# Where the products with v stand: ahead of the next quad's scores instead of behind the row maxima

## The chip, the cores and the metric

The kernel runs on one core of one Trainium2 chip. The metric is the device time of one launch in microseconds, lower is better. Three timed runs of the kernel before gave 1579.79, 1580.98 and 1583.72 us; the median is 1580.98 us. The engines are called TensorE (PE, its weight load PEld), VectorE (DVE), ScalarE (ACT), GpSimd (POOL) and SyncE (SP, which only issues DMAs here).

## The reference

Two layers with the same weights, each made of an attention block and a feed-forward block, in float32, over 2048 rows of 640:

```
x = x + attn(layernorm(x));  x = x + ffn(layernorm(x))      # twice
attn: q, k, v = split(x @ wqkv);  32 heads of 20
      p = softmax(q k^T / sqrt(20), with 0 <= i - j < 256);  (p v) @ wo
ffn:  relu(x @ w1 + b1)^2 @ w2 + b2,   inner size 1536
```

The mask is a sliding window of 256 keys, so a block of 256 queries needs its own keys and those of the block before.

## The kernel before

**Units.** The work is cut into 16 units: 8 blocks of 256 rows in each of 2 layers (`NU` = 16, unit `u`). Large products take each operand as two float16 parts, high and low, and sum three products (`mm3`, L327); this is the dense work. Per unit there are four dense stages: q and k (`stage_qk`), v (`stage_v`), the output projection (`stage_o`) and the feed-forward block (`stage_f`). In unit `u` the kernel runs the attention of unit `u` and, between its parts, the dense stages of others: q, k and v of unit `u + 1`, the output projection and feed-forward block of unit `u - 1`. The last two units have no q, k and v of a later unit left over, so a part of the dense work is held back for them: 18 us of it go from unit 14 to unit 15 (`CARRY`), 20 us from unit 15 to the end (`KEEP`), by the planner's own reckoning.

**Attention.** The 32 heads of a unit are taken four at a time, a quad; a unit has 8 (`NQ`), `n` counts them through all units. Each quad has three runs of small matmuls:

- `max_quad(n)` (L653, in the first block of a layer L668): scores with queries in the partitions, into six PSUM banks `bb`. VectorE adds the mask and takes the maximum of each row (L633). Every second quad the maxima go back as extra rows of q: in most units through a transposing DMA (`max_cross`), in the first two through TensorE (`max_out`).
- `exp_quad(n)` (L757, in the first block L765): scores again with keys in the partitions and the maximum taken off by the extra rows, into the same six banks; ScalarE takes the exponentials (L779) into six buffers `pt`, and GpSimd sets what lies outside the window to zero (L794, L798).
- `pv_quad(n, quad)` (L828): the products of these weights with v, into one of the two PSUM banks that the dense work uses too (`mm_tile`, tag `mm`); ScalarE copies them out (L840), and after every second quad four DMAs on SP write them to the tensor `o` (L845). An extra column of v gives the sums of the weights.

The maxima run three quads ahead (`LEAD` = 3). The six banks `bb` are shared by the maxima and the scores: a run of either waits until the engine that reads the other's result is through (`bbjobs`).

**From `o` to the output projection.** After the first run of scores of unit `u`, `load_o(u - 1)` loads the unit before's `o` and sums from HBM (L871, L872), which waits for all its writes. VectorE divides by the sums (L904, L907), ScalarE and VectorE make the two float16 parts `od` (L911, L914), in four quarters, of which two let the first half of `stage_o` begin. `stage_o` stands in the dense work behind q and half of v.

**The order of the work.** It is written out by a planner that runs while the program is made. It keeps a clock of TensorE (`now`) and of each other engine, with costs in ns for each operation. An instruction of ScalarE, VectorE, GpSimd or SP is a `Job` with what it depends on and a priority; `pump` puts it into its engine's queue when the planner's clock has come to its start. So every engine, SP too, has a fixed order and waits in it. The dense work is a stream of pieces of about 0.5 us of matmuls; a `Want` in it (or before a run of attention) names jobs that must have ended, and by default also that one of the two `mm` banks is free.

`together` (L1104) merges attention and dense work in units 1 to 15. `turns` (L1071) yields two turns per quad: the first with weight 0.55 for the scores, the second with 0.45 for maxima and products with v (0.7 and 0.3 where no maxima are left). Before a turn, `work` (L1112) runs dense pieces until the share of the dense work due by then is done and the turn's wants have ended; if the dense stream itself must wait and the wants have ended, it goes on to the turn at once. With no wants given it has only the share to go by. After the last turn the rest of the dense work of the unit is run, but in units 14 and 15 what lies above the share is left for later. `flow` (L1168) does the same for unit 0: it takes a list of runs in order and puts a piece of dense work between them whenever the next one's wants have not ended.

After unit 15, `load_o(15)` and the unit's output projection, normalisation and feed-forward block follow, with what was kept of the dense work between them.

Of the kernel before, what the change touches and what calls it, by code (L numbers as in the profile page):

```python
# [26 lines left out]
NU = NL * NG  # L27
# [4 lines left out]
NQ = H // 4  # L32
# [13 lines left out]
def kernel(ctx: ExitStack, tc: tile.TileContext, x, wqkv, wo, w1, b1, w2, b2, out):  # L46
# [542 lines left out]
    GQ = NQ // 4  # L589
# [478 lines left out]
    LEAD = GQ + 1  # L1068
    late = []

    def turns(ns, ms, pace=0):  # L1071


        ms = [m for m in ms if m < NQ * NU]
        todo = list(ms)
        for q, n in enumerate(ns):
            m = todo.pop(0) if todo and (q + 1) * max(len(ms), pace) >= (len(ms) - len(todo) + 1) * len(ns) else None
            share = SHARE if m is not None else ALONE
            yield share, ("s", n), None
            yield 1 - share, ("v", n), m  # L1080
        for m in todo:
            yield 1.0, None, m
# [20 lines left out]

    def together(ns, ms, dense, cost, share=1.0, whole=True, after=None, pace=0):  # L1104

        ts = list(turns(ns, ms, pace))
        total = sum(t[0] for t in ts)
        done = part = 0.0
        quad = None
        s = Stream(dense)  # L1110
# [17 lines left out]
        for k, (part_, what, m) in enumerate(ts):  # L1128
            kind = what and what[0]
            wants = list(bbjobs)  # L1130
            if kind == "s" and what[1] % GQ == 0:
                wants.append(rowjobs[what[1] // NQ, what[1] % NQ // GQ])
            if m is not None:
                wants += [trips[m // NQ, j, m % NQ] for j in range(2)]
            if kind == "v":
                wants += quad[1][0]
            work(part, Want(*wants, bank=kind == "v"))
            if kind == "s":
                quad = exp_quad(what[1])
# [27 lines left out]

    def flow(todo, dense):  # L1168

        todo = list(todo)  # L1170
        quad = None
        while todo:
            kind, n = todo[0]
            u, G = n // NQ, n % NQ // GQ
            wants = {"m": [*bbjobs, trips.get((u, 0, n % NQ)), trips.get((u, 1, n % NQ))], "r": mxjobs.get((u, G), [None]),
                     "s": [*bbjobs, *([rowjobs.get((u, G))] if n % GQ == 0 else [])],
                     "v": quad[1][0] if quad else []}[kind]
            if not all(j is not None and j.end is not None and j.end <= now[0] + LOOK for j in wants):
# [13 lines left out]
            elif kind == "s":  # L1192
                quad = exp_quad(n)
# [51 lines left out]
    for u in range(1, NU):  # L1245
        last = u == NU - 1
# [13 lines left out]
        share = 1.0 - KEEP / cost if last else 1.0 - CARRY / cost if u == NU - 2 else 1.0  # L1260
        together(quads, ahead, dense, cost, share, u < NU - 2, after=(lambda: load_o(u - 1, last)) if u > 1 else None, pace=NQ)
    load_o(NU - 1, True)
# [31 lines left out]
```

## Time and profile before

| | |
|---|---|
| median of three timed runs | 1580.98 us (1579.79 to 1583.72) |
| the profiled execution, first to last instruction | 1580.5 us |
| its time beyond that span | not listed; the span lies 0.5 us under the median of the runs |
| TensorE busy | 1555.9 us, 98% |
| VectorE busy | 985.7 us, 62% |
| ScalarE busy | 733.6 us, 46% |
| GpSimd busy | 600.4 us, 38% |
| DMA | 160.44 MB, mean 102 GB/s |
| mean granted clock of TensorE | 0.996 |

In the rows of the profile "L327" is a line of the kernel; a row of the order in time gives start and duration in us, the engine, the line, the operation, what it writes and reads, how many instructions were merged, and in brackets the idle time before it and what ended it. In the list of waits the numbers are us in total, how often, and the longest. A row of a stretch of time, such as 113.90:124.10, gives the length of the stretch, then busy time and count for PE, PEld and, where they are shown, DVE, ACT and POOL, and at the end the granted clock, the share of DMA time and GB/s. Durations of matmuls overlap, so the time of a run is read from the start of one run to the start of the next. The chain of waits merges what ended last into pieces of start, duration, engine and line.

### The profile page before, as it was taken

The page shows a single profiled execution, that of the slowest core. Times are in us where ns is not written, and L with a number is a line of the kernel's source. Part 1 is how long each engine was busy: PE and PEld are TensorE (multiplying, and loading weights), DVE is VectorE, ACT ScalarE, POOL GpSimd, SP SyncE. Part 2 cuts the span into 40 slices and gives each one's busy share as a digit, 9 for nine tenths or more (in the row PEclk, how much of TensorE's full clock was granted, in tenths as well). Part 3 has the DMA queues.
Part 4 walks back from the last instruction along what each step waited for, and adds up shares of the span by engine and source line. Part 5 has one row for each costly group of instructions (what it writes and reads, how often), then busy time and mean ns, then how long its engine had stood idle before and what let it go on. Part 6 is the DMA issues. An engine that isn't in the chain of part 4 may idle for free. (4 is left out here: it accounts for less than half of the span.)

```text
span 1580.5 us, 52541 instructions
## 1 busy us (share of the span) xinstructions
PE 1555.9 (98%) x21570; PEld 1168.6 (74%) x21570; DVE 985.7 (62%) x3254; ACT 733.6 (46%) x1593; POOL 600.4 (38%) x1291
## 2 busy tenths in 40 slices
PE   8989999999999999999999999999999999999999
PEld 7666778777777777777777777777777777676777
DVE  8786765656756656565466756656665576656542
ACT  4565445444454444535444453444535445454522
POOL 1234434235253443524324252443524325344522
PEclk9999999999999999999999999999999999999999
DMA  9763344362533525344353533525354343532120
GB/s 277 200 183 103 78 111 86 100 129 51 123 88 103 112 56 127 79 121 94 89 128 67 123 88 103 112 57 131 76 125 88 89 110 70 124 88 58 30 67 18
DMA packets 243353, 160.44 MB, mean 102 GB/s; under 512 B 91176, under 2 KB 226856, under 8 KB 243112
## 3 DMA queue, kind: packets, MB, share of 16 engines
q1 hardware_dynamic: 236744, 147.58, 39.5%
q10 hardware_dynamic: 6368, 9.50, 2.1%
q8 instruction: 169, 2.77, 0.8%
q14 instruction: 72, 0.59, 0.1%
HBM read 84.68 MB, written 52.95 MB: 87 GB/s over the span
## 5 line engine op out<-in xcount | busy, mean ns | idle before, releaser
L779 ACT ACTIVATE pt<-bb 128x512 f32<-128x512 f32 (+1 forms) x736 | 375.9, 601 | 226.0 <-PE bb L757 198.5
L633 DVE CUSTOM_DVE_ANT_0 bb<-bb,maskq 128x320 f32<-128x320 f32 x896 | 409.2, 524 | 86.8 <-PE bb L653 74.6
L794 POOL TENSOR_SCALAR_AFFINE_SELECT pt<-pt 128x256 f32<-128x256 f32 x448 | 188.3, 422 | 562.7 <-ACT pt L779 549.8
L327 PE MATMUL acc<-y,w_s 128*128 128x256 f16 x2880 | 328.3, 273 | 0.5 <-DVE y L378 0.4
L327 PE MATMUL acc<-w_s,hh 128*128 128x320 f16 (+1 forms) x2340 | 326.4, 298 | 0.0
L327 PEld LDWEIGHTS <-w_s 128*128 128x128 f16 x2880 | 276.6, 98 | 52.1 <-issue 15.8
L327 PEld LDWEIGHTS <-hh 128*128 128x128 f16 x2340 | 222.1, 98 | 96.7 <-issue 11.5
L327 PEld LDWEIGHTS <-wq_s 128*128 128x128 f16 x2400 | 229.5, 98 | 46.1 <-issue 13.6
L327 PE MATMUL acc<-yT,wq_s 128*128 128x256 f16 x2250 | 258.6, 273 | 2.3 <-DVE qd L510 0.9
L798 POOL TENSOR_SCALAR_AFFINE_SELECT pt<-pt 128x256 f32<-128x256 f32 x512 | 213.6, 439 | 89.8 <-ACT pt L779 88.4
L1013 DVE TENSOR_TENSOR hh<-r,hh 128x256 f16<-128x256 f32 x192 | 95.4, 519 | 207.4 <-ACT hh L1010 200.4
L828 PE MATMUL pv<-pt,vt 128*32 128x128 f32 (+1 forms) x3840 | 189.8, 331 | 0.0
L1007 POOL TENSOR_TENSOR r<-r 128x256 f32<-128x256 f32 x192 | 114.2, 615 | 161.4 <-ACT r L1003 159.0
L840 ACT COPY ot<-pv 128x256 f32<-128x256 f32 x128 | 47.6, 372 | 267.0 <-PE pv L828 267.0
L327 PE MATMUL acc<-wo_s,od 128*128 128x320 f16 x960 | 141.6, 304 | 4.8 <-ACT od L911 3.0
L633 DVE DVE_READ_ACCUMULATOR2_ANT mx<- 128x1 f32 x1024 | 144.0, 141 | 0.0
L828 PEld LDWEIGHTS pv<-pt,vt 128*32 128x32 f32 x3840 | 105.5, 110 | 39.2 <-POOL pt L798 4.4
L327 PE MATMUL acc<-wq_s,yT 128*128 128x320 f16 x900 | 132.0, 300 | 1.4 <-DVE y L378 0.9
L327 PEld LDWEIGHTS <-od 128*128 128x128 f16 x960 | 91.9, 99 | 51.0 <-issue 6.4
L1003 ACT ACTIVATE r<-acc,b1s 128x256 f32<-128x256 f32 x192 | 80.5, 471 | 86.7 <-PE acc L327 85.4
L327 PEld LDWEIGHTS <-yT 128*128 128x128 f16 x900 | 85.7, 98 | 39.4 <-issue 6.7
L364 POOL TENSOR_TENSOR bmv<-bmv,neghalf 128x1 f32<-128x1 f32 x64 | 45.5, 717 | 135.8 <-DVE bmv L358 135.4
(95 smaller groups left out, 1226.1 us busy)
## 6 DMA issues: line engine op xcount, KB each, us to landing
qt<-qk SPq DMA_DIRECT2D x30, 480.0 KB
kt<-qk SPq DMA_DIRECT2D x30, 480.0 KB
qk<-qd SPq DMA_DIRECT2D x17, 640.0 KB
o<-ot SPq DMA_DIRECT2D x256, 42.0 KB
od<-o SPq DMA_DIRECT2D x14, 640.0 KB
qk<-yl SPq DMA_DIRECT2D x13, 640.0 KB
qk<-qd SPq DMA_DIRECT2D x17, 320.0 KB
xt<-in_A_x_dram SPq DMA_DIRECT2D x16, 320.0 KB
```

What stands on the lines that cost most here:

```text
L327: nc.tensor.matmul(acc, lhs(a, c), rhs(b, c), start=(k == 0), stop=(k == 3 * nk - 1))
L364: j = post("G", 520, lambda: nc.gpsimd.tensor_tensor(box["mv"][:, 3:4], box["mv"][:, 2:3], neghalf, op=ALU.pow), j, prio=prio)
L633: nc.vector.tensor_tensor_reduce(out=v, in0=v, in1=mask, scale=1.0, scalar=-3.0e38, op0=ALU.add, op1=ALU.max, accum_out=accum[e, w]),
L779: nc.scalar.activation(box["pt"][:, :o], bb[e][:, k, :o], AF.Exp, scale=SCALE / (QS * QS))
L794: nc.gpsimd.affine_select(out=m, in_=m, pattern=[[0, 2], [-1, P]], compare_op=ALU.is_gt, fill=0.0, base=0, channel_multiplier=1)
L798: nc.gpsimd.affine_select(out=m, in_=m, pattern=[[0, 2], [1, P]], compare_op=ALU.is_ge, fill=0.0, base=0, channel_multiplier=-1)
L828: nc.tensor.matmul(pv[32 * jj:32 * (jj + 1), q0 * P:(q0 + qn) * P], vf[:, c:c + 32], pj[:, j, :], start=(k == 0), stop=(k == len(steps) - ...
L840: nc.scalar.copy(ot[:, qd % 2], pv)
L1003: nc.scalar.activation(box["r"], acc[:, f, :], AF.Relu, bias=b1s[:, f0 + f:f0 + f + 1], scale=1.0 / (YS * WS))
L1007: nc.gpsimd.tensor_tensor(box["r"], box["r"], box["r"], op=ALU.mult)
L1013: nc.vector.tensor_sub(hh[:, 1, f, :], box["r"], hh[:, 0, f, :])
```

## The change

The products with v of a quad no longer belong to the turn of the maxima. In `together` they are held in a list `behind` and put out directly ahead of the next quad's scores, after one common wait: for the banks `bb`, for the maxima's rows, for all masks of the quad (before, for those of its first step), and for a free `mm` bank, which the turn of the maxima no longer asks for. The turn of the maxima now has no kind, so the block under `if what is None`, which runs dense work up to the share and then puts out waiting `max_out` calls, applies to it. The last quad of a unit is put out at the first turn of the next; in unit 14 it is put out at the unit's end (`flush`), and the last of unit 15 by `flow`. In unit 0 the list of runs names the products with v of quad `n - 1` ahead of the scores of `n`.

```diff
@@ turns
             share = SHARE if m is not None else ALONE
             yield share, ("s", n), None
-            yield 1 - share, ("v", n), m
+            yield 1 - share, None, m
@@ together(..., flush=False)
                 wants += [trips[m // NQ, j, m % NQ] for j in range(2)]
-            if kind == "v":
-                wants += quad[1][0]
-            work(part, Want(*wants, bank=kind == "v"))
+            values = kind == "s" and bool(behind)
+            if values:
+                wants += [j for ms in behind[0][1][1] for j in ms]
+            work(part, Want(*wants, bank=values))
             if kind == "s":
-                quad = exp_quad(what[1])
+                if values:
+                    pv_quad(*behind.pop())
+                behind.append((what[1], exp_quad(what[1])))
                 for it in late:
                     max_out(*it)
                 late.clear()
...
-            if kind == "v":
-                pv_quad(what[1], quad)
...
+        if flush:
+            work(part, Want(*(j for ms in behind[0][1][1] for j in ms)))
+            pv_quad(*behind.pop())
         work(part, None)
@@ flow(todo, dense, quad=None)
-                     "v": quad[1][0] if quad else []}[kind]
+                     "v": [j for ms in quad[1] for j in ms] if quad else []}[kind]
@@ unit 0
-        todo += [("s", n)] + ([("r", n + LEAD - GQ)] if n % GQ == 1 else []) + [("m", n + LEAD), ("v", n)]
+        todo += [("v", n - 1)] * (n > 0) + [("s", n)] + [("r", n + LEAD - GQ)] * (n % GQ == 1) + [("m", n + LEAD)]
+    todo += [("v", NQ - 1)]
@@ units 1 to 15
-        together(..., pace=NQ)
+        together(..., pace=NQ, flush=u == NU - 2)
+    n, quad = behind.pop()
+    flow([("v", n)], dense, quad)
     load_o(NU - 1, True)
```

More of the change, by code (lines that the diff above doesn't have):

```diff
@@ L1068 @@
     LEAD = GQ + 1
-    late = []
+    late, behind = [], []
     def turns(ns, ms, pace=0):
@@ L1102, in portion, with together @@
             yield c
-    def together(ns, ms, dense, cost, share=1.0, whole=True, after=None, pace=0):
+    def together(ns, ms, dense, cost, share=1.0, whole=True, after=None, pace=0, flush=False):
         ts = list(turns(ns, ms, pace))
@@ L1108, in together @@
         done = part = 0.0
-        quad = None
         s = Stream(dense)
@@ L1166, with flow @@
     QKC, VC, OC, FCST, LNC, CARRY, KEEP, MID = 16.4e3, 8.2e3, 8.2e3, 39.2e3, 1.2e3, 18e3, 20e3, 10e3
-    def flow(todo, dense):
+    def flow(todo, dense, quad=None):
         todo = list(todo)
-        quad = None
         while todo:
@@ L1260 @@
         share = 1.0 - KEEP / cost if last else 1.0 - CARRY / cost if u == NU - 2 else 1.0
-        together(quads, ahead, dense, cost, share, u < NU - 2, after=(lambda: load_o(u - 1, last)) if u > 1 else None, pace=NQ)
+        together(quads, ahead, dense, cost, share, u < NU - 2, after=(lambda: load_o(u - 1, last)) if u > 1 else None, pace=NQ, flush=u == NU - 2)
+    n, quad = behind.pop()
+    flow([("v", n)], dense, quad)
     load_o(NU - 1, True)
```

## The prediction

> **What bounds the kernel now.** I read the page first, then the list of waits, then the order in time of one inner quad, and at the end the last two units and the place where the clock falls.
>
> ```profile
> span 1580.5 us, 52541 instructions
> PE 1555.9 (98%) x21570; PEld 1168.6 (74%) x21570; DVE 985.7 (62%) x3254; ACT 733.6 (46%) x1593; POOL 600.4 (38%) x1291
> PEld pv L828 <- POOL pt L798: 4.4, 20, 0.4
> ```
>
> TensorE has 24.6 us without work in 1580.5. The wait that the change seems to aim at, products with v waiting for masked weights, is 4.4 us in 20 pieces of at most 0.4 us. So there is little to win; the question is whether the new order makes TensorE wait where it now does not. Below, s is a run of scores (L757), m a run of row maxima (L653), v the products with v (L828), "dense" all of L327. An inner quad:
>
> ```profile
> 590.79 0.75 PE L757 MATMUL bb<-qt,kt 62*64 62x192 f16 x32
> 591.63 3.05 ACT L779 ACTIVATE pt<-bb 128x512 f32<-128x512 f32 x6 [4.22 <-PE bb L757]
> 597.03 0.76 PE L653 MATMUL bb<-kt,qt 60*64 60x256 f16 x38
> 602.11 0.14 DVE L633 DVE_READ_ACCUMULATOR2_ANT mx<- 128x1 f32 x1
> 603.08 0.75 PE L757 MATMUL bb<-qt,kt 62*64 62x192 f16 x32
> 590.79:687.36 96.57, 74.85 (x595) 56.80 (x594) 1.00 0.44 97
> ```
>
> The cycle s to s is 12.29 us. It has two latencies: the exponentials end 3.89 us after s starts (then m may overwrite the six banks), and the last maximum is read 5.22 us after m starts (then s may). Both fit, because the planner spreads 595 dense matmuls over the unit's 96.57 us. Here the pace sets the order, not the latency. In the unit before the last (14) less is handed out, and it is the latency that sets it:
>
> ```profile
> 1418.78 0.75 PE L757 MATMUL bb<-qt,kt 62*64 62x192 f16 x32
> 1423.93 0.76 PE L653 MATMUL bb<-kt,qt 60*64 60x256 f16 x38
> 1424.62 1.51 PE L828 MATMUL pv<-pt,vt 128*32 128x256 f32 x32
> 1426.06 2.93 PE L327 MATMUL acc<-y,w_s 128*128 128x256 f16 x25
> 1428.47 0.14 DVE L633 DVE_READ_ACCUMULATOR2_ANT mx<- 128x1 f32 x1
> 1428.92 0.75 PE L757 MATMUL bb<-qt,kt 62*64 62x192 f16 x32
> 1354.04:1439.01 84.97, 61.11 (x495) 47.02 (x494) 1.00 0.38 91
> 1439.01:1511.10 72.09, 47.52 (x366) 34.37 (x365) 1.00 0.16 45
> 1511.10:1580.50 69.40, 64.54 (x540) 50.58 (x540) 1.00 0.15 48
> ```
>
> m to s takes 4.99 us, and s comes 0.31 us after the last maximum is read. Of these 4.99, v covers 1.44 (1424.62 to 1426.06). Unit 14 runs 495 of its 595 matmuls; the other 100 are the carry that covers unit 15 and the end.
>
> **The change, part by part.**
>
> The order itself. Each quad keeps its 32 + 38 + 32 small matmuls; m now goes over to dense, dense to v, v to s. The chain of waits holds this last order already, in the last quads, where no maxima are left:
>
> ```profile
> 1504.10 1.52 PE pv L828 x32
> ```
>
> v, between dense and s, costs 1.52 there against 1.44 in the inner quads. So 0.08 a quad at most, 9 us over 120 quads as an upper bound; but the starts of the runs show that what v gains after dense is lost in the dense run before it, and -0.5 to 2.5 us is left. I take **0**. The masks' wait goes, at most 4.4 us; its pieces are as long as the usual step between two kinds of weight load, so I take **0** here too.
>
> Inner units. [v, s] now go out together, once the maxima are read, the masks are through and a PSUM bank is free. Latency per quad: 3.89 + 5.22 + 1.44 + about 0.5 of rounding = 11.1 us, below 12.29. The pace covers it: **0**. If that cover were gone it would cost 1.44 us a quad. The first [v, s] of a unit brings the last v of the unit before some 4.6 us later against s, and with it the writes of o, their load and the chain to od. SP waits in order for these writes; the loads of x behind them are not urgent.
>
> ```profile
> 590.89 0.41 SPq L872 DMA_DIRECT2D od<-o  x1
> 596.20 0.54 DVE L904 RECIPROCAL rs<-rs 128x64 f32<-128x64 f32 x1
> 605.40 0.49 DVE L914 TENSOR_TENSOR od<-od 128x320 f16<-128x320 f32 x1
> 606.77 2.20 PE L327 MATMUL acc<-wo_s,od 128*128 128x320 f16 x15
> ```
>
> The slack is 606.77 - 605.89 = 0.88 us. Yet the chain stands behind the block of maxima (597 to 602.2) already; only the reciprocal of 0.54 us runs ahead of it. The load, landed by 596.2 now, lands by 600.8 then, still inside the block. So the chain loses 0.54 of 0.88: **0**. The loss if it doesn't hold is a rival below.
>
> First quad of unit 1. TensorE stands here for od, and v of this quad runs inside the hole:
>
> ```profile
> 112.39 0.27 PE L653 MATMUL bb<-kt,qt 60*64 60x256 f16 x1 [1.94 <-ACT pt L779]
> 113.56 2.54 PE L828 MATMUL pv<-pt,vt 128*32 128x256 f32 x32
> 118.38 7.14 PE L327 MATMUL acc<-wo_s,od 128*128 128x320 f16 x30 [2.27 <-ACT od L911]
> 611.03 4.25 PE L327 MATMUL acc<-wo_s,od 128*128 128x320 f16 x30
> 113.90:124.10 10.20, 7.92 (x53) 4.12 (x46) 8.65 (x28) 2.05 (x5) 0.85 (x3) 0.50 1.11 238
> ```
>
> In the new order this v comes with the next s, after the hole, and costs its 1.44 us: **+1.4** (0 to 2.5).
>
> Unit 14. v no longer covers the maxima, so dense fills all of it and then v delays s. From 4.99 the step m to s becomes 4.68 (maximum read) + 0.2 + 1.44 = 6.3: 1.3 us more, in seven of eight quads (after the eighth, v is put out ahead of unit 15 without waiting for the maxima), 9.2 us. Against it, m needs no bank any more. Two quads waited for one:
>
> ```profile
> 1354.73 5.09 PE L327 MATMUL acc<-yT,wq_s 128*128 128x256 f16 x45
> 1354.89 3.04 ACT L779 ACTIVATE pt<-bb 128x512 f32<-128x512 f32 x6 [4.22 <-PE bb L757]
> 1385.85 5.63 PE L327 MATMUL acc<-yT,wq_s 128*128 128x256 f16 x50
> 1386.01 3.05 ACT L779 ACTIVATE pt<-bb 128x512 f32<-128x512 f32 x6 [4.49 <-PE bb L757]
> ```
>
> The dense run goes on 1.9 and 2.4 us past the exponentials; after the share that the pace asks (0.55 of 54.0 / 8 us in the first, nothing more in the other) 1.2 and 2.2 of it are saved. Net 5.9 us of dense more in unit 14 (3 if other quads save too, 9.2 if the bank is waited for at v instead). No time is lost yet: the same work is done earlier. But 43 of the 100 carried matmuls (0.138 us each) are gone, and 57, 7.8 us, are left.
>
> Unit 15, up to its feed-forward part:
>
> ```profile
> 1439.01 1.07 PE L757 MATMUL bb<-qt,kt 62*64 62x192 f16 x32
> 1452.64 0.44 PE L327 MATMUL acc<-wo_s,od 128*128 128x320 f16 x2 [0.71 <-ACT od L911]
> 1453.72 0.45 PE L327 MATMUL acc<-wo_s,od 128*128 128x320 f16 x2 [0.64 <-DVE od L914]
> 1459.84 0.49 DVE L914 TENSOR_TENSOR od<-ov,od 128x320 f16<-128x320 f32 x1 [0.53 <-ACT od L911]
> 1477.78 1.25 PE L327 MATMUL acc<-y,w_s 128*128 128x256 f16 x10 [0.43 <-DVE y L378]
> ```
>
> These are latencies from s at 1439.01: od's first half at 14.7, its second at 21.3, the feed-forward part at 38.8. They stand, as the chain hangs on s and the maxima; the starting s moves to 1445.0. Of the first 14.7 us TensorE can fill 0.7 + 7.8 + 0.7 + 2.1 (s, carry, m, [v, s]) = 11.3. The second half of the output projection (30 matmuls, 4.25 us, with an m between) then ends near 26.5; without carry the normalisation behind it and the transposes are bare, an estimated 7 us (a block of maxima, 4.68, stands on VectorE in their way, and half as much again for their own steps), so the feed-forward part starts at 33.5, that is 1478.5: 0.7 later than now. By then attention is behind by two v (2.9), an s and an m (1.4): **+5.0** (2 to 9).
>
> The end. Unit 15 hands out a fixed 46.6 us of dense before the last v (8.2 + 39.2 + 1.2 + 18 less the kept 20, by the code's constants), however small the carry is, so what is left falls by the same 5.9. It falls by a further 1.75 because the last v now comes after the last 0.3 of a turn (5.8 us a turn):
>
> ```profile
> 1509.67 1.49 PE pv L828 x32
> 1511.16 11.53 PE acc L327 x84
> 1523.21 0.81 DVE od L914 x2
> ```
>
> After the last v 540 matmuls run now; the unit's own are 60 + 360, so 120 (16.4 us) are cover. After the change 8.7, less about 1 by rounding: 7.6. The chain to od takes 12.9 us (1511.16 to 1524.02), 11.53 of it covered; then 7.6, which is 4 us more idle. The 36 matmuls that cover the last normalisation are gone as well, about 3 us: **+7.2** (1.9 to 10.5).
>
> The clock. After idle stretches of 1.94 and 2.27 us around 112 and 117 the profile grants 0.50 for 10.2 us, and thirty matmuls take 7.14 instead of 4.25. I expect idle stretches of 2 to 5 us in unit 15 and at the end; one such event that hits dense work: **+2.9** (0 to 7.8). [...]
>
> Sum: 1.4 + 5.0 + 7.2 + 2.9 = 16.5. On the profiled span 1580.5 that is 1597.0; the median of the runs lies 0.5 above the span, so about **1597.5 us**.
>
> **The rivals.**
>
> A. Not slower: bank waits leave m in most quads of unit 14 and s to m shortens by what m to s gains. It decides itself there: with the carry at 95 or more of the 100 only 1.4 + 1.9 (the last v) remain, 1584 us. For it: the two dense runs that go 1.9 and 2.4 past the exponentials. Against it: in the other quads of the unit I find no such surplus.
>
> B. Faster: the altered first quads of units 0 and 1 happen to close the hole at 112 to 118. Then its 4.2 us of idle (1.94 + 2.27) and 3.9 of half clock (7.14 - 4.25 and 2.54 - 1.51) go and nothing starves: 1573 us. Against it: od there comes from the last v of unit 0, whose place is unchanged.
>
> C. Much slower: in units 2 to 13 od's chain loses the whole 4.6 us of the later load. Less the slack 0.88 and an m of 0.69 pulled forward, 3.0 us for each of twelve units, 36 us: 1617 us or more with the end. It decides from 0.9 us on. Against it: the block of maxima hides the load.
>
> That the change does nothing is no rival outside unit 0: there v is still put out as soon as its masks are through.
>
> **How the numbers follow.** Forecast 0.70, A 0.17, B 0.05, C 0.08. The bounds of the terms, which hang together through the carry, give 1585 to 1608 for the forecast alone; reaching down into A, 1582 to 1608, with B, C and a part of A left out. About 0.3% (4.7 us) can be told from no change. Slower: the forecast and C, 0.78. Same: most of A, 0.15. Faster: B and a little of A, 0.07.
>
> **What would show it.** In the changed profile, units 2 to 13 last 96.6 us as now, s following v by 1.4 us. Unit 14 lasts some 91 us and runs about 540 dense matmuls instead of 495; after the last v come about 475 instead of 540, with 5 us of idle before the matmuls on od, and a window of half clock stands there or in unit 15. I am wrong if unit 14 still runs about 495, if the inner units grow (C), or if the hole at 112 closes (B).

## The result and the profile after

The changed kernel takes **1694.78 us** (median of 4 runs, 1690.99 to 1696.30) against 1580.91 us for the kernel before, a ratio of **1.071** (95% interval 1.0698 to 1.0723). The forecast was 1597.5 with 1608 as its upper end: the direction held, the size did not. The profiled execution took 1690.99 us, with a span of 1689.3, 108.8 more than before. The page of the changed kernel opens with:

```profile
span 1689.3 us, 52604 instructions
PE 1583.3 (94%) x21570; PEld 1176.9 (70%) x21570; DVE 967.2 (57%) x3254; ACT 735.3 (44%) x1593; POOL 591.4 (35%) x1291
```

TensorE runs the same 21570 matmuls and is without work for 106 us instead of 24.6. Its busy time, too, has grown by 27.4 us: some of the matmuls ran on a lower clock (the mean of the profiled execution is 0.975, where it was 0.996). Counting only gaps above 60 ns, the idle time of TensorE rose from 21.4 to 102.8 us; the time at half clock rose from 13.7 to 85.3 us, and what that cost (an estimate, half of the working time inside it) from 5.7 to 31.4. The 81.4 and the 25.7 together are 107.1 of the 108.8 us. In the list of waits of the changed kernel two waits of the matmuls for `od` are the longest, and those of the transposes of maxima are among the next:

```profile
PE acc L327 <- DVE od L914: 38.3, 12, 3.5
PE acc L327 <- ACT od L911: 26.5, 14, 10.1
PE tr L721 <- DVE mx L633: 7.1, 3, 4.6
```

Twelve waits, eleven of them of 3.39 to 3.52 us, where the output projection stands for a subtraction that makes the low part of `od`: nothing of that length was in the list before. The stretches from the first scores of a unit to those of the next show where the time went; of the changed kernel unit 1, an inner unit, and unit 15 with the end (length, then busy time and count of each engine, and at the end the granted clock, the DMA share and GB/s):

```profile
107.44:222.84 115.40, 95.84 (x1314) 67.98 (x1314) 67.95 (x217) 48.44 (x103) 39.37 (x84) 0.93 0.35 85
527.54:629.91 102.37, 98.45 (x1414) 73.19 (x1410) 59.04 (x198) 45.26 (x98) 37.95 (x84) 0.98 0.39 92
1527.86:1689.30 161.44, 130.18 (x1531) 96.31 (x1530) 59.77 (x180) 53.25 (x120) 48.20 (x100) 0.89 0.13 39
```

and of the kernel before unit 1 (unit 15 and the end stand in the prediction, in two pieces that make 141.5 us):

```profile
108.40:206.70 98.30, 91.86 (x1298) 65.67 (x1297) 68.43 (x216) 47.43 (x103) 42.49 (x84) 0.95 0.42 101
```

| stretch | before | after | more |
|---|---|---|---|
| before unit 1 | 108.4 | 107.4 | -1.0 |
| unit 1 | 98.3 | 115.4 | 17.1 |
| units 2 to 13 (unit 8: 87.8 in both) | 1147.3 | 1209.2 | 61.9 |
| unit 14 | 85.0 | 95.8 | 10.9 |
| unit 15 and the end | 141.5 | 161.4 | 19.9 |

**An inner unit.** The inner units lose most, and they were forecast at nothing. Unit 6 of the changed kernel in order of time, rows of TensorE, VectorE and ScalarE together, cut to what the reading needs:

```profile
629.91 0.75 PE L757 MATMUL bb<-qt,kt 62*64 62x192 f16 x32
636.16 0.76 PE L653 MATMUL bb<-kt,qt 60*64 60x256 f16 x38
636.85 2.90 PE L327 MATMUL acc<-yT,wq_s 128*128 128x256 f16 x25
638.78 0.69 DVE L510 SCALAR_TENSOR_TENSOR qd<-acc,qd 128x512 f16<-128x512 f32 x1 [0.36 <-ACT qd L507]
640.25 0.42 DVE L510 SCALAR_TENSOR_TENSOR qd<-acc,qd 128x256 f16<-128x256 f32 x1
641.89 0.14 DVE L633 DVE_READ_ACCUMULATOR2_ANT mx<- 128x1 f32 x1
642.41 1.51 PE L828 MATMUL pv<-pt,vt 128*32 128x256 f32 x32
643.85 0.75 PE L757 MATMUL bb<-qt,kt 62*64 62x192 f16 x32
646.53 2.51 PE L327 MATMUL acc<-wo_s,od 128*128 128x320 f16 x15 [0.34 <-ACT od L911]
648.60 0.87 ACT L911 CAST od<-od 128x320 f16<-128x320 f32 x2
649.89 0.50 DVE L633 CUSTOM_DVE_ANT_0 bb<-bb,maskq 128x320 f32<-128x320 f32 x1 [0.32 <-PE bb L653]
653.81 0.14 DVE L633 DVE_READ_ACCUMULATOR2_ANT mx<- 128x1 f32 x1
655.01 0.47 DVE L914 TENSOR_TENSOR od<-od 128x320 f16<-128x320 f32 x1
655.53 3.58 PE L327 MATMUL acc<-wo_s,od 128*128 128x320 f16 x13 [3.39 <-DVE od L914]
```

The same places in the unit of the kernel before that the prediction showed (scores at 590.79):

```profile
601.09 0.69 DVE L510 SCALAR_TENSOR_TENSOR qd<-acc,qd 128x512 f16<-128x512 f32 x1
607.81 0.88 ACT L911 CAST od<-od 128x320 f16<-128x320 f32 x2
608.36 1.09 DVE L914 TENSOR_TENSOR od<-od 128x320 f16<-128x320 f32 x2 [0.99 <-ACT od L911]
609.77 0.48 DVE L633 CUSTOM_DVE_ANT_0 bb<-bb,maskq 128x320 f32<-128x320 f32 x1
```

Two things are to be seen. First, the second scores come later. Before, v ran right behind m, and for 1.44 us no dense tile ended; only one eviction (an operation that takes a finished tile out of its PSUM bank, here into `qd`, 601.09) got in among the eight reductions, just before the last. Now dense work runs right behind m, a tile ends inside the block, and VectorE, in the order that the planner wrote, runs two evictions between the reductions and even waits 0.36 us for ScalarE with reductions behind it. The last maximum is read at 642.03 (12.1 us after the scores) instead of 602.25 (11.5), and as v and s now both come after it, the next scores start after 13.94 us (643.85 - 629.91) instead of 12.29. Of these 1.65 us the longer block makes 0.65 (12.12 for 11.46); the rest is v and the end of a dense run, which stood beside the block and now stand behind it.

Second, the last two subtractions for `od` stood just ahead of the second block of maxima (608.36 and 609.77). The casts of ScalarE that they need come behind the exponentials of the second scores and move with them: they end 19.56 us after the first scores (649.47) instead of 17.90 (608.69). The block moves by 1.0 us only, from 18.98 to 19.98 (649.89). In the planner's order the subtractions now come behind it, the second ends at 655.48, and TensorE stands for 3.39 us. In this turn nothing else is offered to it: the turn of maxima has no kind any more, and the block under `if what is None` insists on its share of dense work, whose next piece is the one that waits.

At the end of this hole the clock falls from 1.00 to 0.50; a stretch of the changed kernel:

```profile
655.50:658.92 3.42, 3.38 (x13) 1.79 (x13) 0.86 (x3) 0.00 (x0) 0.55 (x1) 0.50 0.02 5
```

Thirteen matmuls at 0.50 take 3.5 us (655.53 to 659.04) in place of 1.94 (the same thirteen at 1.00 in unit 9, 947.43 in the last section): 1.6 us. So unit 6 loses 3.92 us to idle time (0.53 of it in small waits) and 1.6 to the clock, of 5.8.

**The last two units.** Single rows from the changed kernel's order in time, and its stretches counted for L327 alone (length, busy time and count for PE, PEld, then the clock):

```profile
1511.74 0.76 PE L653 MATMUL bb<-kt,qt 60*64 60x256 f16 x38
1518.86 0.75 PE L757 MATMUL bb<-qt,kt 62*64 62x192 f16 x32
1539.70 4.44 PE L327 MATMUL acc<-wo_s,od 128*128 128x320 f16 x19 [7.14 <-ACT od L911]
1617.20 1.26 PE L327 MATMUL acc<-w_s,hh 128*128 128x320 f16 x8
1628.56 9.95 PE L327 MATMUL acc<-wo_s,od 128*128 128x320 f16 x60 [10.11 <-ACT od L911]
```

```profile
1432.04:1527.86 95.82, 74.06 (x590) 56.41 (x590) 1.00 0.35 86
1617.26:1689.30 72.04, 52.62 (x428) 40.92 (x428) 0.88 0.13 41
```

In unit 14 the step m to s is 7.12 us in this quad (1511.74 to 1518.86), where it was 4.99 in the same quad before; over the first seven quads of the unit it is 6.05 to 9.88, 7.8 on average, where it was 5.6. And 590 dense matmuls run there: the carry of 100 is used up to the last few. So TensorE stands 7.14 us in unit 15 for `od`, and after the last v only 8 matmuls are there to cover the chain to `od`: 10.11 us more, and the first 3.15 of the 9.95 us that its 60 matmuls take run at half clock (1628.56 to 1631.71).

### The profile page after: what moved, and what is told of

It reads as the page before. It is cut to its first block, busy times and chain, and to the rows that moved or that the text cites. A ratio compares the mean times of both kernels' runs of the same rounds, so it can differ in the third digit from the quotient of the medians.

```text
span 1689.3 us, 52604 instructions
## 1 busy us (share of the span) xinstructions
PE 1583.3 (94%) x21570; PEld 1176.9 (70%) x21570; DVE 967.2 (57%) x3254; ACT 735.3 (44%) x1593; POOL 591.4 (35%) x1291
## 4 chain that ended last, share of the span: by engine, by line
PE 85%; DVE 7%; ACT 2%; DMA 2%; issue 2%; SPq 1%; POOL 0%; DVEq 0%; ACTq 0%; POOLq 0%
PE acc L327 65%; PE pv L828 10%; PE bb L653 5%; PE bb L757 4%; DVE bb L633 3%; ACT pt L779 1%; DVE od L914 1%; DVE mx L633 1%; DVE bst L353 1%; DMA qk<-qd 0%; DMA x<-in_A_x_dram 0%; DMA od<-o 0%; PE spin L341 0%; DMA ov<-o 0%; PE bb L765 0%
## 5 line engine op out<-in xcount | busy, mean ns | idle before, releaser
L794 POOL TENSOR_SCALAR_AFFINE_SELECT pt<-pt 128x256 f32<-128x256 f32 x448 | 183.9, 411 | 726.9 <-ACT pt L779 711.0
L327 PE MATMUL acc<-y,w_s 128*128 128x256 f16 x2880 | 335.8, 276 | 2.0 <-DVE y L378 1.4
L327 PE MATMUL acc<-w_s,hh 128*128 128x320 f16 (+1 forms) x2340 | 326.1, 298 | 0.0
L327 PEld LDWEIGHTS <-w_s 128*128 128x128 f16 x2880 | 278.1, 99 | 46.0 <-issue 3.0
L327 PEld LDWEIGHTS <-hh 128*128 128x128 f16 x2340 | 221.9, 98 | 88.9 <-issue 1.1
L327 PE MATMUL acc<-yT,wq_s 128*128 128x256 f16 x2250 | 258.2, 274 | 2.5 <-DVE qd L510 0.8
L327 PEld LDWEIGHTS <-wq_s 128*128 128x128 f16 x2400 | 231.7, 98 | 37.6 <-issue 3.8
L798 POOL TENSOR_SCALAR_AFFINE_SELECT pt<-pt 128x256 f32<-128x256 f32 x512 | 207.1, 426 | 96.6 <-ACT pt L779 85.7
L327 PE MATMUL acc<-wo_s,od 128*128 128x320 f16 x960 | 163.4, 328 | 68.5 <-DVE od L914 38.3
L828 PE MATMUL pv<-pt,vt 128*32 128x128 f32 (+1 forms) x3840 | 184.0, 329 | 2.3 <-DVE y L378 1.2
L327 PEld LDWEIGHTS <-od 128*128 128x128 f16 x960 | 95.9, 106 | 127.6 <-DVE od L914 48.6
L327 PE MATMUL acc<-wq_s,yT 128*128 128x320 f16 x900 | 132.4, 300 | 1.1 <-DVE y L378 0.6
L327 PEld LDWEIGHTS <-yT 128*128 128x128 f16 x900 | 85.5, 98 | 36.1 <-issue 1.9
```

Of the source, the lines that this page charges most:

```text
L327: nc.tensor.matmul(acc, lhs(a, c), rhs(b, c), start=(k == 0), stop=(k == 3 * nk - 1))
L794: nc.gpsimd.affine_select(out=m, in_=m, pattern=[[0, 2], [-1, P]], compare_op=ALU.is_gt, fill=0.0, base=0, channel_multiplier=1)
L798: nc.gpsimd.affine_select(out=m, in_=m, pattern=[[0, 2], [1, P]], compare_op=ALU.is_ge, fill=0.0, base=0, channel_multiplier=-1)
L828: nc.tensor.matmul(pv[32 * jj:32 * (jj + 1), q0 * P:(q0 + qn) * P], vf[:, c:c + 32], pj[:, j, :], start=(k == 0), stop=(k == len(steps) - ...
```

## The experiments

Theories, as they came up: `od`'s subtractions lose their place in VectorE's order to the next block of maxima because the second scores come late (T1 in the expectations); the load of `o` is late, as rival C has it (T2); the turn of maxima suffers from having no kind (T3); the common wait of v and s holds both back (part of T1); early load and untied v are needed together (T4); v behind m shields the block of maxima from evictions (T5); the whole inner hole is the place of the last two subtractions (T6). Diffs are against the changed kernel, unless another is named. A time without a ratio is that of one profiled execution.

**Give the turn of maxima a kind of its own**, so that the block under `if what is None` no longer applies to it.

```diff
-            yield 1 - share, None, m
+            yield 1 - share, ("m", n), m
```

> The turn of the maxima gets a kind of its own again, so that dense work up to the share is no longer forced behind it and waiting max_out calls go out after the next scores as before; the rest of the change stays. Three theories on the inner units, which grew from 96.57 to 102.4 us with one idle stretch of 3.39 us ahead of the second half of the output projection. T1 (order on VectorE: with v tied to the maxima, s of the second quad comes 1.65 us later and its maxima 0.7 us sooner after it, so the last two quarters of od fall behind that block of maxima): idle stretch stays at 2 to 3.4 us, units at 100 to 102.4. T2 (the unit's first [v, s] makes the load of o 4 us later): the same, no change. T3 (TensorE stands only because the turn has no way on while dense work is blocked): [v, s], 2.1 us, go into the hole, idle 1.3 us or less, no half clock, units at 97 to 98. Unit 1 (115.4 us against 98.3): if the forced order of max_out is its cause, back to 98 to 104.

1661.95 us, 32.8 less. Unit 1, and the longest wait of scores, in this run:

```profile
109.90:214.70 104.80, 92.68 (x1313) 66.61 (x1312) 69.32 (x217) 47.82 (x103) 41.78 (x84) 0.95 0.37 93
```

```profile
PE bb L757 <- DMA qt<-mt: 9.9, 7, 2.9
```

Unit 1 gets 10.6 of its 17.1 us back: the waits of transposes for maxima (L721) fall from 7.1 to 0.2 us. The waits for `od`'s subtraction fall from 38.3 to 5.9 us, and in the inner units the hole of 3.39 us is gone; but they still last 99.0 to 101.9 us, as scores now wait up to 2.9 us for the maxima and their rows. Unit 14 is unchanged (95.8 us), unit 15 with the end nearly so (159.6). So the missing kind is one cause of several.

**The load of `o` earlier.** First, the last v of every unit at the unit's end:

```diff
-        together(..., flush=u == NU - 2)
+        together(..., flush=u < NU - 1)
```

> The last products with v of every unit are put out at the end of that unit, as the change does in unit 14 alone, so the writes and the load of o are as early as before. T2 (late load): units 3 to 13 back to 96.6 to 97.5 us, span 1625 to 1640. T1 (spacing of s and maxima inside the unit): the load is early, but the second block of maxima still goes ahead of od's last quarters; units stay at 100 to 102.5. T3: no change, 102.4.

1693.71 us; most inner units 102.37 as in the changed kernel. It told nothing: the flush stands behind all dense work of the unit, so the load (L872) is still issued 3.9 to 5.6 us after the first scores, as in the changed kernel. Then the last v in its old place, behind the last maxima of the unit:

```diff
+            values, edge = kind == "s" and bool(behind), flush and k == len(ts) - 1
+            if values or edge:
+                wants += [j for ms in behind[0][1][1][:1 if edge else None] for j in ms]
+            work(part, Want(*wants, bank=values or edge))
...
+            if edge:
+                pv_quad(*behind.pop())
```

> In units 1 to 14 the products with v of the unit's last quad stay where they were before the change, behind that quad's turn of maxima, so the writes and the load of o start some 4 us sooner against the next unit's first scores; all other products with v lead the next scores, waiting for the maxima too. (Putting them at the very end of the unit had left the load at 2.9 to 3.9 us after the first scores, so that run did not test it.) T2 (the late load is what makes od late): units 3 to 13 at 96.6 to 98 us, no idle ahead of the second half of the output projection. T1 (v tied to the maxima, s of the second quad 1.65 us later): the hole of 3.39 us stays, units at 101 to 102.4. T4 (both together: each alone pushes od's last quarters over the edge of the block of maxima): also 101 to 102.4 here, and only the run with both undone comes back. Unit 14 and 15 as in the changed kernel in all cases (95 us; 25 to 28 us of idle).

1687.89 us. Unit 5's load and hole, and the stretches of units 5 and 6:

```profile
527.83 0.43 SPq L872 DMA_DIRECT2D od<-o  x1
552.65 1.94 PE L327 MATMUL acc<-wo_s,od 128*128 128x320 f16 x13 [3.39 <-DVE od L914]
```

```profile
527.27:627.78 100.51, 96.81 (x1412) 72.58 (x1412) 59.21 (x198) 45.35 (x98) 38.29 (x84) 1.00 0.39 93
627.78:729.91 102.13, 98.42 (x1412) 73.18 (x1411) 59.12 (x198) 45.36 (x98) 38.30 (x84) 0.98 0.39 92
```

The load is issued 0.6 us after the first scores instead of some 4.0, and the hole is 3.39 us all the same. So the late load is not the cause of this hole; with it falls the mechanism that rival C named. The two units have the same idle time (3.70 us) and differ in the clock alone: the event costs 1.62 us.

**v without the maxima**: v waits for its masks and a bank only, then s for the rest.

```diff
-            values = kind == "s" and bool(behind)
-            if values:
-                wants += [j for ms in behind[0][1][1] for j in ms]
-            work(part, Want(*wants, bank=values))
+            if kind == "s" and behind:
+                work(part, Want(*[j for ms in behind[0][1][1] for j in ms]))
+                pv_quad(*behind.pop())
+            work(part, Want(*wants, bank=False))
```

> Products with v wait for their masks and a bank alone, the scores behind them for the maxima; order and place stay. So v can cover the maxima again. T1: s of the second quad comes at the pace (12.3 us after the first), od's last quarters get ahead of the maxima, units 3 to 13 at 96.6 to 97.5. T2: the load is as late as in the changed kernel, 102.4 stays. Either way, if tying v to the maxima is what lengthened unit 14 (95.8 us and 590 dense matmuls against 85.0 and 494), that unit comes back to 85 to 88 us and 490 to 520, and the idle time of unit 15 and the end falls from 28.2 us to 3 to 8.

1655.13 us, 39.7 less. Units 5, 10, 11 and 14:

```profile
521.94:624.34 102.40, 99.09 (x1414) 73.69 (x1410) 59.64 (x198) 45.44 (x98) 38.34 (x84) 0.97 0.39 92
1017.49:1117.17 99.68, 96.37 (x1414) 72.60 (x1410) 59.81 (x198) 45.50 (x98) 38.43 (x84) 1.00 0.40 94
1117.17:1218.47 101.30, 97.99 (x1414) 73.29 (x1410) 59.72 (x198) 45.44 (x98) 38.38 (x84) 0.98 0.40 93
1419.46:1504.68 85.22, 85.22 (x1326) 63.80 (x1322) 53.65 (x183) 43.64 (x97) 38.10 (x82) 1.00 0.38 93
```

Unit 14 is back at 85.2 us with 506 dense matmuls, and unit 15 with the end gains 12.7 (148.7 us): there the common wait is the cause, as the prediction's step had it. The inner units keep their hole (3.31 us), which here one subtraction makes: the second scores come 12.99 us after the first, still 0.7 later than before, the first of the two late subtractions gets ahead of the block and the second does not. So untying v is not enough. With this same hole a unit lasts 99.68, 101.30 or 102.40 us, and the clock in these rows is 1.00, 0.98 and 0.97.

**Own kind and untied v together**, the first and the last diff:

> The turn of maxima with a kind of its own (no forced dense work) and v not tied to the maxima; the load stays late. T3 and the tie together explain all: units 3 to 13 at 96.6 to 98. T2 or T4 (late load): some 98.5 to 101, as the hole is filled but od's last quarters stay behind the maxima. Unit 14 at 85 us; unit 1 at 101 to 105.

1606.62 us, so the two undo 84 of the 109 us of span. Unit 1 is at 99.3, unit 14 at 85.2, unit 15 with the end at 147.0; an inner unit:

```profile
498.86:597.11 98.25, 96.48 (x1416) 72.53 (x1412) 59.56 (x198) 45.44 (x98) 38.34 (x84) 1.00 0.42 96
```

One hole of 1.77 us is left in each inner unit, still for the last subtraction, behind the second block of maxima, and in the unit shown no half clock follows it (1.00). With the last v of the units moved back as well:

> The early load of the run before, and v no longer tied to the maxima. T2 and T4: units 3 to 13 at 96.6 to 97.5 us without idle. T1: also, since v is untied, but that is out already if untying alone left 102.4. T3 (only the forced dense work makes TensorE stand): still 99 to 102. Unit 14 at 85 to 86 us, idle of unit 15 and the end 5 to 8 us.

> All three undone: own kind, untied v, last v of a unit in its old place. What is left of the change is the place of v, ahead of the next scores instead of behind the maxima, in seven of eight quads. If the three explain the loss: 1579 to 1590 us, units 3 to 13 at 96.5 to 96.8, unit 14 at 85 to 86. If the place itself costs (other steps between kinds of matmuls, 0 to 0.08 us a quad): up to 1600.

Untied v with the edge: 1644.18 us with the hole of 3.39 us. All three: 1625.08 us, ratio 1.0278 (1.0254 to 1.0302); this missed what was expected. Here scores wait up to 3.3 us for the maxima's rows, ahead of the place where the hole for `od` was. The DMAs of these rows leave at nearly the same time as without the edge (from 18.4 and 18.3 us after the first scores in unit 5), so why the edge brings this wait stays open.

**The place of `od`'s operations in VectorE's order.** The priority of all of them raised, in the changed kernel and in the one with own kind and untied v:

```diff
-            pr = 2 if u else 1
+            pr = 0        # and, in two more kernels, pr = 1
```

> All instructions that make od get the first priority in the planner, ahead of the maxima; nothing else differs from the changed kernel. T1 and T2 (order on VectorE decides, whatever made od late): the idle stretch of 3.39 us goes, units 3 to 13 at 96.6 to 98 us, no half clock there. If the data of o itself lands too late, the idle stretch stays at over 2 us. Unit 14 stays at 94 to 97 us, unit 15 and the end keep over 20 us of idle time.

> The changed kernel with that priority alone; v still tied to the maxima and the dense share still forced. T6: the stretch of 3.39 us goes, units 3 to 13 at 96.6 to 99 us (the first half of od still 0.5 late), but unit 1 stays at 112 to 116, unit 14 at 95 to 96 and unit 15 with the end at 158 to 162: 1640 to 1660 us in all. If od's place does not matter: 1685 to 1695.

> As the run with a kind of its own and untied v (1604.9 us, units 98.2 with one hole of 1.77 us ahead of od's second half), and od's instructions posted with the priority of the maxima, so that in its turn the older entry goes first. T6 (od's casts for the last two quarters come some 1 us later than before the change, 18.2 against 17.0 us after the unit's first scores, and so miss the place ahead of the second block of maxima; only that makes the hole): units 3 to 13 at 96.5 to 97, no idle, in all 1583 to 1592 us. If the hole comes from something else in od's chain: 1600 to 1607.

Priority 0: 1692.31 us; priority 1: 1664.57 us in the changed kernel, 1621.76 us with own kind and untied v, ratio 1.0250 (1.0231 to 1.0268). Each time the hole of 3.39 us (or 1.77) for the late subtractions is gone. In the changed kernel that gains 2 and 30 us, and in the one with own kind and untied v 15 us are lost all the same: `od`'s other operations now stand inside the first block of maxima, in its inner units the next scores come 17.4 to 20.4 us after the first instead of 12.3, and in three of them the maxima wait 2.7 us for exponentials. All three times missed what was expected; the runs show only that the wait goes when its place in the order goes. Raising the reductions and exponentials above all else instead, beside own kind and untied v, went the other way, with evictions of dense tiles behind the block:

```diff
-    urgency = {"out": 0, "turn": 1}
+    urgency = {"out": 0, "turn": 0}
```

> As the run with a kind of its own and untied v, and the maxima and exponentials in the first priority, so that no eviction of a dense tile breaks into a block of maxima. T5 (before the change v stood between the maxima and the dense tile and kept that tile's eviction out of the block; now it falls into it, the block ends 12.0 us after the unit's first scores instead of 11.4, and the second scores come at 13.0 instead of 12.3): second scores at 12.2 to 12.5, od's last quarters ahead of the next block, units 3 to 13 at 96.5 to 97.5. If the block is not what delays od: the hole of 1.77 us stays, 98.2.

1651.12 us, against 1606.62 without it; inner units 100.3 with stalls of 1.5 and 0.9 us for evictions. In unit 6 no eviction breaks the first block of maxima any more (it ends 10.8 us after the first scores), but TensorE waits for the evictions put off, the next scores come after 13.96 us, and `od`'s last two subtractions stand behind the second block again. So a whole block alone does not bring `od` back. The clean form moves the two late subtractions alone (own kind and untied v beside it):

```diff
-            js.append(post("D", 402, low, j, prio=pr))
+            js.append(post("D", 402, low, j, prio=min(pr, 1) if i > 1 else pr))
```

> As the run with a kind of its own and untied v (1604.9 us, units 98.24 us, one hole of 1.77 us ahead of the second half of od). Only the two last subtractions of od, 0.5 us each on VectorE, get the priority of the maxima, so they go ahead of the younger block. T6 (nothing but these two, behind the block, makes the hole): holes gone, units 3 to 13 at 96.5 to 97.2, 1584 to 1590 us in all. If the second half of od waits for more than that (casts, load, reciprocal): holes of 1 us or more stay, 1595 to 1606.

1590.65 us, ratio 1.0054 (1.0036 to 1.0072), just above the expected 1584 to 1590. Unit 6 of this kernel, VectorE and then the whole unit, and unit 15 with the end:

```profile
610.26 1.16 DVE L914 TENSOR_TENSOR od<-od 128x320 f16<-128x320 f32 x2
611.35 0.49 DVE L633 CUSTOM_DVE_ANT_0 bb<-bb,maskq 128x320 f32<-128x320 f32 x1
```

```profile
591.49:687.80 96.31, 96.31 (x1416) 72.62 (x1412) 59.22 (x198) 45.48 (x98) 38.49 (x84) 1.00 0.40 98
1444.64:1591.70 147.06, 138.35 (x1631) 103.12 (x1630) 62.01 (x183) 53.02 (x120) 49.56 (x100) 0.98 0.15 45
```

The two subtractions are ahead of the block again, and TensorE is never without work in the unit. Six inner units last 96.31 us; four (5, 7, 10 and 11) have short waits of scores for the maxima's rows instead, 0.7 to 1.1 us in all. That names the cause of the hole that was left: one instruction of about 0.5 us on the wrong side of a block of 4 us. In the changed kernel it is two, and there the hole for them went when their priority was raised with the rest of `od`'s.

**The shield, in the kernel before.** v stays behind the maxima there, but three dense pieces are put between the two:

```diff
@@ the kernel before, after the maxima, ahead of v
+                for _ in range(3):
+                    c = s.go()
+                    done += c or 0.0
+                work(part, Want())
```

> The kernel before, with three pieces of dense work (some 1.6 us) put between the maxima and the products with v behind them; v still stands behind the maxima of its turn and covers part of them, and nothing else is changed. T5 (v right behind the maxima keeps the next eviction of a dense tile out of their block on VectorE): the block of the unit's first maxima breaks as in the changed kernel and ends 12.0 us after the first scores instead of 11.4, and units 3 to 13 grow by up to 1.8 us. If only the wait of [v, s] and the forced dense share cost: 96.6 us, as before.

1617.46 us, 35 more than the kernel before, from this alone. Its block of maxima in unit 6 (scores at 598.01):

```profile
606.88 0.69 DVE L510 SCALAR_TENSOR_TENSOR qd<-acc,qd 128x512 f16<-128x512 f32 x1 [0.36 <-ACT qd L507]
608.34 0.42 DVE L510 SCALAR_TENSOR_TENSOR qd<-acc,qd 128x256 f16<-128x256 f32 x1
609.98 0.14 DVE L633 DVE_READ_ACCUMULATOR2_ANT mx<- 128x1 f32 x1
```

The block is broken by the same two evictions, with the same wait of 0.36 us, and ends 12.1 us after the scores, as in the changed kernel. So it is shown that v right behind m keeps the second eviction out of the block. It is not shown that the longer block makes the hole for `od`: in this unit the second scores come after 12.40 us, both late subtractions stay ahead of the second block, and TensorE does not wait for them. That this edit costs 35 us was not expected; it also makes v itself later, and how the 35 us divide (inner units at 98.0 to 100.7 us, with waits of maxima for exponentials; 7.3 us in the last unit and the end) was not followed further.

**The rest of the loss.** The kernel of the two late subtractions, with v in its old place in units 14 and 15:

```diff
+            old_v = old and kind == "m"
+            if old_v:
+                wants += behind[0][1][1][0]
+            work(part, Want(*wants, bank=old_v))
...
+            if old_v:
+                pv_quad(*behind.pop())
...
+        together(..., old=u >= NU - 2)
```

(and the `od` that is read in unit 8 left out of the raised priority).

> As the run with its own kind, untied v and the two last subtractions of od moved up (1590.7 us), with two differences: in units 14 and 15 the products with v stand where they stood before the change, right behind the maxima, and in the unit after a layer's first (whose o chain is shorter) the subtractions keep their priority. If the rest of the loss is only where v stands in the last two units (unit 14 in that run 85.9 us, unit 15 with the end 147.1 against 85.0 and 141.5) and the 2.3 us of unit 8: 1578 to 1583 us, the same as the kernel before; inner units at 96.31, unit 8 at 87.8, unit 15 with the end at 141 to 143. If the last units suffer from something the inner ones leave them: 1585 or more. A gain over the kernel before of at most 0.26 us for each inner unit, 3 us in all.

1583.86 us (11 runs) against 1582.01 (15 runs), ratio 1.0012 (1.0003 to 1.0021), which is below the 0.3% that can be told from no change. An inner unit, and unit 15 with the end:

```profile
592.33:688.63 96.30, 96.30 (x1414) 72.56 (x1411) 59.20 (x198) 45.47 (x98) 38.42 (x84) 1.00 0.40 98
1440.13:1582.10 141.97, 135.04 (x1627) 101.97 (x1626) 62.87 (x184) 52.69 (x120) 49.59 (x100) 1.00 0.16 46
```

The end is back at 142.0 us from 147.1, unit 14 at 85.1 from 85.9, unit 8 at 87.8 from 90.1. So of the 9.6 us of span that this run gains on the one before, v's place in the last two units gives 5.9 and the priority in unit 8 gives 2.3. In the inner units v leads the next scores at no cost: without unit 7 they last 96.3 to 97.2 us, 96.52 on average, against 96.57. No version beat the kernel before.

## Why the prediction was right or wrong

**The order itself (0): right.** With the side effects gone the inner units take 96.52 us on average against 96.57, so v between dense work and s costs nothing that these runs can show.

**The masks' wait (0): right** in sum; no version shows a gain that could be put down to it.

**The inner units (0): wrong, and the largest error**: 61.9 us. The step that failed is "So the chain loses 0.54 of 0.88: 0". It followed `od`'s first half only; in the changed kernel that half does wait no more than 0.34 us. The second half was not looked at: its last two subtractions stood directly ahead of a block of maxima, and the casts that they need came 1.66 us later, the block only 1.0. The runs that leave the priorities of `od` and of the maxima alone bear this out (units 4, 6, 9 and 12): with 1.09 to 1.30 us between the last cast and the block, in the kernel before and its edited form, both subtractions get ahead of it; with 0.57, where v is untied and not moved back, one does; with 0.53 or less, as in the changed kernel (0.42), none. Nor did the step "latency per quad 11.1 us, below 12.29" hold, and for two reasons. It lets m start when the exponentials end, 3.89 us after s; but the share of dense work puts m at 6.25 us, in the kernel before (597.03) as in the changed one (636.16). With m there, the old 5.22 us up to the last maximum and 1.44 for v already make 12.9 us. And it took the block of maxima at its old length. The block gets longer when dense tiles end inside it, which the edit in the kernel before shows by itself, and this cycle became 13.94. The third thing missed is that the block under `if what is None` takes away the way out, and so turned a late `od` into idle time. Rival C had the right place and sign, but the wrong cause (an earlier load left the hole as it was) and half the size: 3.0 us a unit against 5.8 in unit 6 (3.92 idle, 1.6 clock, the rest small steps).

**First quad of unit 1 (+1.4): wrong**, 17.1 in the whole unit. The hole at 112 to 118 did stay open. But the transposes of the maxima's rows, put out at the end of a turn without kind, made TensorE wait up to 4.59 us for VectorE; the own kind gave 10.6 us back, and untied v with it nearly all (99.3 against 98.3). The prediction did not price the block under `if what is None` at all.

**Unit 14 (540 matmuls, 91 us): mechanism right, size off**, 590 and 95.8. The mis-sized term is the step m to s: 6.3 us forecast from an unbroken block, 7.12 measured in the quad of the prediction, where an eviction gets into the block and the last maximum is read after 5.28 us instead of 4.68, and 7.8 on average. The bank that m no longer needs was to save 3.3 us of dense work; the cycle of a quad grew by 1.36 us in spite of it (10.85 / 8). Untying v brought the unit back to 506 and 85.2.

**Unit 15 and the end (+5.0 and +7.2, +2.9 for the clock): mechanism right, size off**, +19.9. It follows from the carry: 57 of 100 matmuls were to be left, almost none were. A wait of 7.14 us in unit 15, and one of 10.11 us after the last v where "5 us of idle" were forecast, with 428 matmuls behind that v instead of 475.

**The clock (+2.9): right in kind, too few events.** One event was counted; the clock cost 25.7 us more in all. The event that can be told apart costs 1.62 us (100.51 and 102.13 us above, in units with the same idle time), less than the 2.9 taken from a stretch of 10.2 us.

**Rivals A and B** did not come about: the carry fell to almost nothing, and the hole in unit 1 grew (3.27 us for `od`). The direction was right because of the steps on the last units, which the runs bear out; the range failed because it gave rival C 0.08 and left its time out, on the sight of one half of a chain.

## What to carry to other kernels

Before a run of matmuls is moved, look at what its old place kept apart on the other engines: here 1.44 us of TensorE work that ended no dense tile kept an eviction out of a block of reductions. Three dense pieces ahead of it cost 35 us in 1582, of which it is not shown how much comes from that eviction. Follow a chain to its last instruction, not to the first that lets work begin, and ask what stands next in that engine's fixed order: slack there isn't used up little by little, for a small operation that misses its place waits for the whole block (here 0.5 us behind 4, which left a hole of 1.77 us on TensorE, and two of them one of 3.39). Work held back to cover the end is eaten by every us by which the cycle grows in the unit that holds it back, and the idle time that took its place here brought half clock with it (0.89 on average over unit 15 and the end).

## What the runs showed of the hardware

A hole of 3.31 to 3.52 us on TensorE goes with half clock sometimes and sometimes not. In the kernel with untied v the units with the same hole of 3.31 us had a clock of 1.00 (unit 10), 0.98 (unit 11) and 0.97 (unit 5) in the rows above. In the changed kernel eleven inner units have a hole of 3.39 to 3.52 us for `od`. In ten of them a stretch at 0.50 begins 0.02 to 0.45 us ahead of the hole's end and lasts 3.41 us; in unit 9 there is none. Nor do shorter holes of this kernel go by their length: one of 2.62 us stays at 1.00, and one of 1.86 us has half clock 0.75 us behind it. These two and the hole of unit 9, and the stretches of the changed kernel in which they lie or which follow them (length, busy time and count of PE, PEld, DVE, ACT and POOL, clock, DMA share, GB/s):

```profile
236.58 0.45 PE L327 MATMUL acc<-wo_s,od 128*128 128x320 f16 x2 [2.62 <-ACT od L911]
947.43 1.94 PE L327 MATMUL acc<-wo_s,od 128*128 128x320 f16 x13 [3.39 <-DVE od L914]
1559.29 0.74 PE L391 MATMUL tr<-ident,xt 128*128 128x128 f32 x5 [1.86 <-DVE xt L366]
233.96:242.90 8.94, 5.43 (x71) 3.48 (x70) 7.18 (x19) 4.66 (x10) 3.85 (x8) 1.00 0.75 172
943.00:951.00 8.00, 4.61 (x69) 2.82 (x71) 5.75 (x21) 0.10 (x1) 0.55 (x1) 1.00 0.08 13
1560.04:1566.86 6.82, 5.90 (x45) 3.97 (x48) 0.89 (x2) 2.52 (x6) 3.84 (x8) 0.50 0.08 20
```

In unit 1 of the kernel before, the half clock starts at 113.88, 1.49 us behind the hole of 1.94 us and ahead of the hole of 2.27:

```profile
113.88:124.11 10.23, 7.95 (x53) 4.14 (x46) 8.67 (x28) 2.05 (x5) 0.87 (x3) 0.50 1.11 238
```

The stretches at 0.50 inside the span are 3.41, 6.83 or 10.24 us long: 11, 4 and 2 of them in the changed kernel, one of 3.41 and one of 10.24 in the kernel before. With own kind and untied v, the inner unit shown has a hole of 1.77 us and a clock of 1.00, and the whole execution 0.996. So the length of a hole alone does not tell whether half clock comes; what does is not shown by these runs.
